# Attention and gated MLP in one kernel: a first chunk of four query tiles, a second of two, and weight low parts split between VectorE and GpSimd

## The chip, the cores and the metric

The kernel runs on one core of a Trainium2 chip. The metric is the device time of one execution in microseconds (us), the median of several runs; smaller is better.

## The reference, cut to what matters

```python
# q, k, v: (4, 8, 768, 64) float32; n_sink = 4; window = 128
scores = scale * np.matmul(q, k.transpose(0, 1, 3, 2))
is_sink = pos[None, :] < int(n_sink)
rel = pos[:, None] - pos[None, :]
in_window = (rel >= 0) & (rel < int(window))
scores = np.where(is_sink | in_window, scores, -1000000000.0)
a = np.exp(scores - max); a = a / (sum(a) + 1e-09)
attn = np.matmul(a, v)                      # sliding window and sinks
x = attn.transpose(0, 2, 1, 3).reshape(3072, 512)
out = ((x @ w_a) * (x @ w_b)) @ w_out       # 512 -> 1536 -> 512, weights float64
```

## The kernel before, in words

A query tile is 128 rows of one batch. There are 4 batches of 6 tiles, so 24 tiles, and a **chunk** is some tiles of one batch: before, eight chunks of three tiles, in the order batch 0 first half, batch 1 first half, batch 0 second half, batch 1 second half, and the same for batches 2 and 3. A chunk is written here as (batch, first tile, number of tiles).

For each chunk two things are done. **Attention** goes through 8 heads times the tiles of the chunk; one head with one tile is a **unit**. A unit's scores `s` (one window of 264 keys: 128 before, 8 sinks, 128 of its own; only 128 keys for tile 0 of a batch) are made by TensorE (PE), masked and reduced by VectorE (DVE), put through exp by ScalarE (ACT), scaled, transposed by PE, copied by ACT, and multiplied with `v` on PE (`av`); the sinks' part (`skt`, `sk`) is added once for a pair or four of heads. **MoE**, the gated product, multiplies the chunk's `x` with the weights in 12 rounds `j`: a half `a` (12 matmuls), a half `b` (12 matmuls), the product `g` (DVE), its split into a high part `gh` (ACT) and a low part `gl` (GpSimd, called POOL in the rows; in the last round DVE), and the projection `o` of the round before (9 matmuls for three tiles). Every MoE matmul is made of three: high times high, high times low, low times high.

The float64 weights are not split on the host. Each of the 36 weight tiles (`a`, `b`, `o` of 12 rounds) is loaded raw and prepared once, while it is first needed: `weight_bits` (two integer operations on DVE, L278 and L283, one conversion, L282 on ACT or L280 on GpSimd, one add on GpSimd, L285), `weight_high` (a cast on ACT, L292) and `weight_low` (a subtraction, L297, on GpSimd for the first five weights and on DVE for the other 31). All of this falls into the attention of chunk 0, which runs alone, and into the MoE of chunk 0.

The MoE of chunk c runs with the attention of chunk c+1 woven in: `between` takes steps of a generator after each half and each projection. I call this **stage c**; the attention of chunk 0 ahead of it is the **prologue**. In the prologue the first weight step is taken at step 17 of the attention and then every second step, 7 in all. Attention of chunks 0 and 1 is "exact": its matmuls take float32 operands as they are. From chunk 2 on, k, q and v are split into a high and a low part on GpSimd first (L325, L328), two instructions each. In chunk 1 heads 3, 5 and 7 have k and q split in this way too.

The order on each engine comes from a scheduler, but each engine then works strictly in its order, so an instruction that waits holds up all behind it on that engine.

Of the kernel before, what the change touches and what calls it, by code (L numbers as in the profile page):

```python
# [192 lines left out]

class Fast:
# [653 lines left out]
```

## Time and profile before

| | us |
|---|---|
| median of 3 runs | 825.75 (824.84 to 828.64) |
| the profiled execution, its own time | 826.2 |
| its span, first to last instruction | 824.4 |
| PE busy in the span | 789.7 (96%) |
| DVE busy | 439.8 (53%) |
| ACT busy | 480.0 (58%) |
| GpSimd busy | 392.9 (48%) |
| mean granted TensorE clock | 0.982 |

The busy shares are means over a span with two very different parts: the time until the weights are prepared, and the rest. They are read by stretches in what follows. A busy PE is also not a PE at its peak, since matmuls overlap and their ends are modelled; the spacing of matmul starts tells more.

### The profile page before, as it was taken

The numbers are of one execution on the slowest core, as the hardware profiler recorded it, in microseconds if no ns is written. First come the engines' busy times: TensorE is split into PE (matmuls) and PEld (weight loads), VectorE is DVE, ScalarE is ACT, GpSimd is POOL, SyncE is SP. The second block draws the span as 40 slices with busy tenths as digits, with TensorE's granted clock in tenths as the row PEclk, the third lists the DMA queues.
The fourth block names the chain that finished last, engine by engine and source line by source line (L and its number), as shares of the span: only waits on it lengthen the run. The fifth ranks groups of instructions, "written<-read, shape, count | busy, mean of one in ns | idle before, by whom it ended". The sixth has DMA issues, their size and how long they took to land.

```text
span 824.4 us, 13568 instructions
## 1 busy us (share of the span) xinstructions
PE 789.7 (96%) x4453; PEld 716.5 (87%) x4453; DVE 439.8 (53%) x1435; ACT 480.0 (58%) x1403; POOL 392.9 (48%) x469
## 2 busy tenths in 40 slices
PE   8888989989999999999999999999999999999995
PEld 5567767879999999999999999999999999999994
DVE  6999899625553456535654455535554456431001
ACT  5657757436764677647664577647775677631111
POOL 2375767736564367425545256426646256201110
PEclk9989989989999999999999999999999999999998
DMA  8855620221121133331333123332333132000001
GB/s 300 323 178 185 223 91 27 66 93 46 49 62 43 52 99 115 101 100 49 101 119 106 52 91 111 114 97 62 110 109 114 52 97 59 1 22 18 1 1 44
DMA packets 44785, 75.89 MB, mean 92 GB/s; under 512 B 4640, under 2 KB 25760, under 8 KB 44704
## 3 DMA queue, kind: packets, MB, share of 16 engines
q1 hardware_dynamic: 41648, 69.42, 26.5%
q10 hardware_dynamic: 3024, 5.51, 1.8%
q8 instruction: 37, 0.61, 0.3%
q14 instruction: 44, 0.36, 0.1%
q0 software_dynamic: 32, 0.00, 0.0%
HBM read 68.62 MB, written 6.29 MB: 91 GB/s over the span
## 4 chain that ended last, share of the span: by engine, by line
PE 80%; DVE 13%; ACT 2%; POOL 2%; issue 1%; DMA 0%; DVEq 0%; POOLq 0%; ACTq 0%
PE o L662 22%; PE b L653 21%; PE a L653 21%; PE s L399 4%; PE t L431 4%; PE av L447 4%; DVE wf_a L278 1%; PE av L576 1%; DVE w_o L297 1%; DVE wf_b L278 1%; DVE wf_a L283 1%; DVE g L674 1%; PE s L525 1%; DVE wf_o L283 1%; DVE p L533 1%
## 5 line engine op out<-in xcount | busy, mean ns | idle before, releaser
L653 PE MATMUL a<-xh,w_a 128*128 128x384 f32 x768 | 221.9, 349 | 1.2 <-DVE st L533 1.2
L653 PE MATMUL b<-xh,w_b 128*128 128x384 f32 x768 | 218.3, 345 | 0.0
L662 PE MATMUL o<-w_o,gh 128*128 128x512 f32 x576 | 188.6, 407 | 1.0 <-ACT gh L677 1.0
L679 POOL TENSOR_TENSOR gl<-g,gh 128x384 fp32r<-128x384 f32 x88 | 91.7, 1042 | 194.8 <-ACT gh L677 194.1
L653 PEld LDWEIGHTS a<-xh,w_a 128*128 128x128 f32 x768 | 142.8, 192 | 3.0 <-DVE st L533 1.4
L653 PEld LDWEIGHTS b<-xh,w_b 128*128 128x128 f32 x768 | 141.7, 190 | 0.5 <-issue 0.3
L674 DVE TENSOR_TENSOR g<-b,g 128x384 f32<-128x384 f32 x96 | 53.4, 556 | 155.3 <-PE b L653 150.9
L653 PE MATMUL a<-xl,w_a 128*128 128x384 f32 x384 | 130.9, 341 | 2.0 <-DVE xl L635 2.0
L653 PE MATMUL b<-xl,w_b 128*128 128x384 f32 x384 | 129.9, 338 | 0.0
L662 PEld LDWEIGHTS o<-w_o,gh 128*128 128x128 f32 x576 | 104.9, 190 | 19.9 <-ACT gh L677 1.8
L662 PE MATMUL o<-w_o,gl 128*128 128x512 f32 x288 | 114.9, 399 | 2.2 <-POOL gl L679 2.2
L677 ACT CAST gh<-g 128x384 fp32r<-128x384 f32 x96 | 49.3, 514 | 86.3 <-DVE g L674 86.0
L670 ACT COPY g<-a 128x384 f32<-128x384 f32 x96 | 45.2, 471 | 79.1 <-PE a L653 68.7
L410 ACT ACTIVATE p<-p,st 128x264 f32<-128x264 f32 (+1 forms) x144 | 72.2, 502 | 25.8 <-DVE st L409 24.8
L406 ACT ACTIVATE p<-p,st 128x264 f32<-128x264 f32 (+1 forms) x144 | 72.4, 503 | 9.2 <-DVE st L404 9.2
L434 ACT CAST pt<-t 128x256 fp32r<-128x256 f32 (+1 forms) x144 | 51.3, 356 | 44.5 <-PE t L431 42.8
L653 PEld LDWEIGHTS a<-xl,w_a 128*128 128x128 f32 x384 | 73.8, 192 | 3.6 <-DVE xl L635 2.3
L653 PEld LDWEIGHTS b<-xl,w_b 128*128 128x128 f32 x384 | 73.1, 190 | 0.0
L404 DVE CUSTOM_DVE_ANT_0 p<-s,mg 128x264 f32<-128x264 f32 x112 | 48.0, 429 | 45.2 <-PE s L399 45.1
L662 PEld LDWEIGHTS o<-w_o,gl 128*128 128x128 f32 x288 | 54.7, 190 | 16.0 <-POOL gl L679 2.6
L435 DVE TENSOR_TENSOR pt<-t,pt 128x256 fp32r<-128x256 f32 (+1 forms) x144 | 58.2, 404 | 18.2 <-ACT pt L434 16.7
L328 POOL TENSOR_TENSOR ks<-kr,ks 64x536 fp32r<-64x536 f32 (+1 forms) x51 | 63.9, 1254 | 4.2
(142 smaller groups left out, 1305.4 us busy)
## 6 DMA issues: line engine op xcount, KB each, us to landing
qr<-in_qT_dram SPq DMA_DIRECT2D x51, 192.0 KB, 2.4
raw_a<-in_wa_dram SPq DMA_DIRECT2D x12, 512.0 KB, 5.9
raw_b<-in_wb_dram SPq DMA_DIRECT2D x12, 512.0 KB, 6.6
raw_o<-in_wo_dram SPq DMA_DIRECT2D x12, 512.0 KB, 6.9
chk_a<-in_wa_dram SPq DMA_DIRECT2D x24, 256.0 KB, 2.7
chk_b<-in_wb_dram SPq DMA_DIRECT2D x24, 256.0 KB, 2.7
chk_o<-in_wo_dram SPq DMA_DIRECT2D x24, 256.0 KB, 2.8
out_dram<-os ACTq DMA_DIRECT2D x21, 256.0 KB, 2.1
```

Source lines behind the costliest of these rows:

```text
L328: self.nc.gpsimd.tensor_tensor(o, i, high.bitcast(F32), op=ALU.subtract)
L404: nc.vector.tensor_tensor_reduce(out=p[:, :w], in0=ps[:, :w], in1=m, scale=-0.125, scalar=BIG, op0=ALU.add, op1=ALU.min, accum_out=st[:, 0:1])
L406: nc.scalar.activation(p[:, :w], p[:, :w], AF.Exp, bias=st[:, 0:1], scale=-1.0, accum_out=st[:, 1:2])
L410: nc.scalar.mul(p[:, :w], p[:, :w], st[:, 3:4])
L434: nc.scalar.copy(hs, tp[:, :n, :])
L435: nc.vector.tensor_tensor(ls, tp[:, :n, :], hs.bitcast(F32), op=ALU.subtract)
L653: nc.tensor.matmul(ps[:, :n], lhsT=w[:, ksl], rhs=x[:, :n], start=kk == 0 and i == 0, stop=kk == NK - 1 and i == 2)
L662: nc.tensor.matmul(outs[i], lhsT=g[:, sl], rhs=w, start=j == 0 and k == 0, stop=j == NJ - 1 and k == 2)
L670: nc.scalar.copy(g[:, :n], pa[:, :n])
L674: nc.vector.tensor_tensor(g[:, :n], pb[:, :n], g[:, :n], op=ALU.mult)
L677: nc.scalar.copy(gh[:, :n], g[:, :n])
L679: e.tensor_tensor(gl[:, :n], g[:, :n], gh[:, :n].bitcast(F32), op=ALU.subtract)
```

## The change

The chunks become (0,0,4), (0,4,2), (1,0,3), (2,0,3), (1,3,3), (2,3,3), (3,0,3), (3,3,3): chunk 0 has four tiles, chunk 1 the other two of batch 0, the rest three each. In the prologue the k, q and v of two heads instead of one are loaded ahead, and the weight steps begin at step 18 and come every third step, again 7. No head of chunk 1 is split on GpSimd. Of the low parts every third weight's (all of kind `b`) goes to GpSimd, all others to DVE, and the conversion L282 is always on ACT. The copies of the sink columns `sc` go from DVE to GpSimd for chunks 0 and 1. `gl` of the last two rounds of a chunk is on DVE. In chunk 1 the transposed tile and the `av` product share one PSUM bank, since the fourth output tile of chunk 0 takes the bank `av`. The output staging tiles use the buffers of `gh` and `gl`.

```diff
-POOL_FIRST = 5
-STEP0, STEPS = 17, 2
+POOL_LOW = (1, 3)
+STEP0, STEPS = 18, 3
-SPLIT_KQ = (3, 5, 7)
+CHUNKS = ((0, 0, 4), (0, 4, 2), (1, 0, 3), (2, 0, 3), (1, 3, 3), (2, 3, 3), (3, 0, 3), (3, 3, 3))
...
-    def early(self, kind, j):
-        return 3 * j + "abo".index(kind) < POOL_FIRST
+    def low_engine(self, kind, j):
+        return self.nc.gpsimd if (3 * j + "abo".index(kind)) % POOL_LOW[1] == POOL_LOW[0] else self.nc.vector
...
-        if self.early(kind, j):
-            nc.gpsimd.tensor_scalar(lo, lo.bitcast(U32), 2.0 ** -29, 1.0, op0=ALU.mult, op1=ALU.mult)
-        else:
-            pin(nc.scalar.activation(lo, lo.bitcast(U32), AF.Copy, scale=2.0 ** -29))
+        pin(nc.scalar.activation(lo, lo.bitcast(U32), AF.Copy, scale=2.0 ** -29))
...
-        e = self.nc.gpsimd if self.early(kind, j) else self.nc.vector
+        e = self.low_engine(kind, j)
...
-                nc.vector.tensor_copy(sc[h // 2, i][:, h % 2, :], p[:, P:P + NS])
+                nc.gpsimd.tensor_copy(sc[h // 2, i][:, h % 2, :], p[:, P:P + NS])
...
-        do_prep(0)
+        for h in range(early):
+            do_prep(h)
...
-        outs = [self.ps.tile([P, DM], F32, tag=f"o{i}", name=f"o{tag}_{i}") for i in range(nt)]
+        outs = [self.ps.tile([P, DM], F32, tag=("o0", "o1", "o2", "av")[i], name=f"o{tag}_{i}") for i in range(nt)]
...
-            e = nc.vector if j == NJ - 1 else nc.gpsimd
+            e = nc.vector if j >= NJ - 2 else nc.gpsimd
...
-            o = self.mo.tile([P, DM], F32, tag="os", bufs=3, name=f"os{tag}_{i}")
+            o = self.mo.tile([P, DM], F32, tag=("gh", "gl")[i % 2], name=f"os{tag}_{i}")
...
-        chunks = [(b, t0, 3) for b0 in range(0, B, 2) for t0 in (0, 3) for b in (b0, b0 + 1)]
+        chunks = CHUNKS
...
-                gen = self.attention(nb, nt0, nnt, nxf, exact=c == 0, split=SPLIT_KQ)
+                gen = self.attention(nb, nt0, nnt, nxf, exact=c == 0)
```

GpSimd's order in the middle of stage 0, around the low part `gl` of round 5, before (`wf_o6` is the add for weight `o` of round 6; `ks`, `qh`, `ql` with 5 are the split k and q of head 5 of chunk 1):

```order
L285 TENSOR_TENSOR wf_o6_1183<-wf_o6_1183,raw_o6_985 128x512
L285 TENSOR_TENSOR wf_a7_1232<-wf_a7_1232,raw_a7_1004 128x512
L325 TENSOR_SCALAR ks1_5_0_1250<-kr1_5_0_1246 64x400
L328 TENSOR_TENSOR ks1_5_0_1250<-kr1_5_0_1246,ks1_5_0_1250 64x400
L325 TENSOR_SCALAR qh1_5_0_1251<-qr1_5_0_1248 128x384
L285 TENSOR_TENSOR wf_b7_1275<-wf_b7_1275,raw_b7_1042 128x512
L328 TENSOR_TENSOR ql1_5_0_1252<-qr1_5_0_1248,qh1_5_0_1251 128x384
L679 TENSOR_TENSOR gl0_5_1333<-g0_5_1293,gh0_5_1332 128x384
```

The same place in the changed program (`w_b6` is the low part of weight `b` of round 6, `sc` the sink copies):

```order
L689 TENSOR_TENSOR gl0_4_1297<-g0_4_1255,gh0_4_1296 128x512
L282 TENSOR_TENSOR wf_a7_1305<-wf_a7_1305,raw_a7_1113 128x512
L546 COPY sc0_4_4_0_1335<-p0_4_4_0_1328 128x8
L294 TENSOR_TENSOR w_b6_1348<-wf_b6_1237,w_b6_1348 128x512
L282 TENSOR_TENSOR wf_b7_1350<-wf_b7_1350,raw_b7_1152 128x512
L546 COPY sc0_4_4_1_1379<-p0_4_4_1_1372 128x8
L282 TENSOR_TENSOR wf_o7_1389<-wf_o7_1389,raw_o7_1180 128x512
L689 TENSOR_TENSOR gl0_5_1409<-g0_5_1368,gh0_5_1408 128x512
```

Between two `gl` there are now three adds, one low part and two small copies in every round; before there were three adds, and in three of the rounds the four operations that split a head.

GpSimd's order at the end of stage 0, before (`gl0_10` is the low part of round 10; `qh`, `ql`, `vv`, `vs` ahead of it are the last of some fourteen split operations for heads 0, 1 and 4 of chunk 2):

```order
L325 TENSOR_SCALAR vv0_1_3_2042<-vr0_0_3_2005 128x4x64
L328 TENSOR_TENSOR ql0_1_3_2037<-qr0_1_3_2033,qh0_1_3_2036 128x384
L328 TENSOR_TENSOR vv0_1_3_2042<-vr0_0_3_2005,vv0_1_3_2042 128x4x64
L325 TENSOR_SCALAR vs0_4_3_2371<-vsr0_4_3_2369 128x256
L328 TENSOR_TENSOR vs0_4_3_2371<-vsr0_4_3_2369,vs0_4_3_2371 64x256
L679 TENSOR_TENSOR gl0_10_1880<-g0_10_1849,gh0_10_1879 128x384
```

And in the changed program, the corresponding place:

```order
L325 TENSOR_TENSOR vv1_0_0_2029<-vr1_0_0_2027,vv1_0_0_2029 128x3x64
L689 TENSOR_TENSOR gl0_9_1826<-g0_9_1801,gh0_9_1825 128x512
L322 TENSOR_SCALAR vs1_0_0_2034<-vsr1_0_0_2032 128x256
L325 TENSOR_TENSOR vs1_0_0_2034<-vsr1_0_0_2032,vs1_0_0_2034 64x256
L322 TENSOR_SCALAR vv1_1_0_2064<-vr1_0_0_2027 128x3x64
L325 TENSOR_TENSOR vv1_1_0_2064<-vr1_0_0_2027,vv1_1_0_2064 128x3x64
L322 TENSOR_SCALAR qh1_1_0_2058<-qr1_1_0_2055 128x384
L294 TENSOR_TENSOR w_b11_1857<-wf_b11_1783,w_b11_1857 128x512
```

The split operations for chunk 2 stood ahead of `gl` of round 10; `gl` of round 10 is no longer on GpSimd, and the same kind of operations now stands ahead of `gl` of round 9 and of the low part `w_b11`.

## Rows read from the trace of the kernel before

**Rows 1.** Windows: length, busy of PE, PEld, DVE, ACT, POOL; clock, DMA share, GB/s.
```profile
100.00:140.00 40.00, 35.73 (x190) 31.41 (x189) 36.36 (x80) 27.02 (x67) 27.73 (x22) 0.91 0.24 74
180.00:220.00 40.00, 40.00 (x246) 37.97 (x244) 20.70 (x81) 27.01 (x82) 22.89 (x29) 1.00 0.16 43
```

**Rows 2.** Starts of rounds 1 and 11, then of stages 1, 2, 3, 4: start, us.
```profile
52.52 0.90 PE L653 MATMUL a<-xh,w_a 128*128 128x384 f32 x1
162.25 0.34 PE L653 MATMUL a<-xh,w_a 128*128 128x384 f32 x1
176.68 0.52 PE L653 MATMUL a<-xh,w_a 128*128 128x384 f32 x1
271.67 0.34 PE L653 MATMUL a<-xh,w_a 128*128 128x384 f32 x1
366.85 0.34 PE L653 MATMUL a<-xh,w_a 128*128 128x384 f32 x1
458.55 0.34 PE L653 MATMUL a<-xh,w_a 128*128 128x384 f32 x1
```

**Rows 3.** DVE's weight operations: start, us, line, operation, count.
```profile
31.12 0.69 DVE L283 SCALAR_TENSOR_TENSOR wf_b<-raw_b,wf_b 128x512 int32<-128x512 int32 x1
...
36.48 1.45 DVE L278 TENSOR_SCALAR wf_a<-raw_a 128x512 int32<-128x512 int32 x1
...
157.86 0.67 DVE L297 TENSOR_TENSOR w_b<-wf_b,w_b 128x512 fp32r<-128x512 f32 x1
```

**Rows 4.** GpSimd: an add, a low part `gl`, the split of one head.
```profile
36.37 1.28 POOL L285 TENSOR_TENSOR wf_o<-wf_o,raw_o 128x512 int32<-128x512 int32 x1
...
97.13 1.01 POOL L679 TENSOR_TENSOR gl<-g,gh 128x384 fp32r<-128x384 f32 x1 [1.98 <-ACT gh L677]
...
102.72 0.85 POOL L325 TENSOR_SCALAR ks<-kr 64x400 fp32r<-64x400 f32 x1
103.66 1.13 POOL L328 TENSOR_TENSOR ks<-kr,ks 64x400 fp32r<-64x400 f32 x1
104.87 0.83 POOL L325 TENSOR_SCALAR qh<-qr 128x384 fp32r<-128x384 f32 x1
...
107.35 1.20 POOL L328 TENSOR_TENSOR ql<-qr,qh 128x384 fp32r<-128x384 f32 x1
```

**Rows 5.** DVE groups until 177 us: count, busy us, mean ns, idle before.
```profile
L297 DVE TENSOR_TENSOR w_a<-wf_a,w_a 128x512 fp32r<-128x512 f32 x10 | 10.0, 1005 | 0.0
...
L547 DVE COPY sc<-p 128x8 f32<-128x8 f32 x16 | 5.6, 351 | 2.0 <-ACT p L542 1.9
```

**Rows 6.** Chain that ended last: start, us, line, matmuls in the piece.
```profile
11.27 1.24 PE av L576 x10
...
13.44 0.45 PE s L525 x2
13.88 0.11 PE t L562
...
189.60 2.08 PE a L653 x12
...
195.48 2.11 PE o L662 x9
...
389.91 0.59 PE av L447 x5
```

**Rows 7.** The prologue on DVE: first unit, first weight step.
```profile
6.39 0.29 DVE L533 CUSTOM_DVE_ANT_0 p<-s,m 128x128 f32<-128x128 f32 x1
...
26.65 0.41 DVE L278 TENSOR_SCALAR wf_a<-raw_a 128x512 int32<-128x512 int32 x1
```

**Rows 8.** End of stage 0 on GpSimd and on PE.
```profile
168.16 0.99 POOL L679 TENSOR_TENSOR gl<-g,gh 128x384 fp32r<-128x384 f32 x1
...
169.21 0.50 PE L662 MATMUL o<-w_o,gl 128*128 128x512 f32 x1 [2.17 <-POOL gl L679]
```

**Rows 9.** Windows: stage 3, columns as in rows 1.
```profile
366.80:458.50 91.70, 91.63 (x531) 85.43 (x531) 46.27 (x175) 57.36 (x180) 45.02 (x63) 1.00 0.31 93
```

More of the change, by code (lines that the diff above doesn't have):

```diff
@@ L369, in prep_v, with attention @@
         return vv
-    def attention(self, b, t0, nt, xf, exact=False, split=(), alone=False):
-        parts = self.parts_exact(b, t0, nt, xf, split, alone) if exact else self.parts_split(b, t0, nt, xf)
+    def attention(self, b, t0, nt, xf, exact=False, alone=False):
+        parts = self.parts_exact(b, t0, nt, xf, alone) if exact else self.parts_split(b, t0, nt, xf)
         late = [i for i in range(nt) if t0 + i >= 2]
         units = [(h, i) for h in range(H) for i in range(nt)]
-        return self.pipeline(units, nt, late, *parts, 3 if alone else 2, 2 if exact else 4)
+        return self.pipeline(units, nt, late, *parts, 3 if alone else 2, 2 if exact else 4, 2 if alone else 1)
     def parts_split(self, b, t0, nt, xf):
@@ L476, in parts_split, with parts_exact @@
         return do_prep, scores, transposes, av, sinks_t, sinks_av
-    def parts_exact(self, b, t0, nt, xf, split, alone):
+    def parts_exact(self, b, t0, nt, xf, alone):
         nc = self.nc
@@ L523, in scores @@
             ps = self.ps.tile([P, SW], F32, tag="sa"[n % 2] if alone else "s", name=f"s{u}")
[L524 to L526 removed]
+            nc.tensor.matmul(ps[:, :w], lhsT=q[:, i * P:(i + 1) * P], rhs=k[:, c0:c0 + w], start=True, stop=True)
             if alone and n % 5 > 2:
@@ L590, in sinks_av, with pipeline @@
             n = len(late)
-            ps = self.ps.tile([P, 3 * P], F32, tag="av", name=f"sk{tag}_{pr}")
-            nc.tensor.matmul(ps[:, :n * P], lhsT=vss[pr], rhs=skt.pop(pr)[:, :n * P], start=True, stop=True)
-            xs = xf[pr][:, late[0] * P:nt * P]
-            nc.vector.tensor_tensor(xs, ps[:, :n * P], xs, op=ALU.add)
+            if alone:
+                ps = self.ps.tile([P, 4, P], F32, tag="av", name=f"sk{tag}_{pr}")
+            else:
+                ps = half_bank(1, f"sk{tag}_{pr}")
+            nc.tensor.matmul(ps[:, :n, :], lhsT=vss[pr], rhs=skt.pop(pr)[:, :n * P], start=True, stop=True)
+            xs = xf[pr][:, late[0] * P:nt * P].rearrange("p (c q) -> p c q", q=P)
+            nc.vector.tensor_tensor(xs, ps[:, :n, :], xs, op=ALU.add)
         return do_prep, scores, transposes, av, sinks_t, sinks_av
-    def pipeline(self, units, nt, late, do_prep, scores, transposes, av, sinks_t, sinks_av, lag, group):
-        do_prep(0)
+    def pipeline(self, units, nt, late, do_prep, scores, transposes, av, sinks_t, sinks_av, lag, group, early):
+        for h in range(early):
+            do_prep(h)
         yield
@@ L712, in run @@
         b, t0, nt = chunks[0]
-        xf = self.new_xf(0)
+        pairs = [self.wp.tile([P, 2, nt * P], F32, tag=f"w_{k}{NJ - 1}", name=f"xf0_{k}") for k in "bo"]
+        xf = [x[:, i, :] for x in pairs for i in range(2)]
         first = self.attention(b, t0, nt, xf, exact=True, alone=True)
```

116 lines of the change are left out of this document (60 added, 56 removed).

## The prediction

> **What bounds the kernel now.** I read the windows first. From 100 to 140 us DVE is busy 36.4 of 40 us and PE's clock is granted at 0.91 on average, so it partly ran at the lower of its two levels; from 180 to 220 us DVE is busy 20.7, PE all 40 and the clock is full [rows 1]. So there are two regimes: PE bounds the kernel from the end of stage 0 on, and before that PE waits for prepared weights. Then the starts of rounds: in stage 0 ten rounds take 162.25 - 52.52 = 109.7 us, 10.97 each; stage 1 takes 271.67 - 176.68 = 95.0, stage 2 95.2 and stage 3 91.7 us [rows 2]. Stage 3 is shorter because the attention woven into it is of tiles 0 to 2, whose first tile has half a window; stages 1 and 2 carry tiles 3 to 5. The end of stage 0 shows one wait of its own: PE stands 2.17 us for `gl` of round 10, which GpSimd does at 168.16, behind the split operations of chunk 2 [rows 8]. From the start of round 11 to stage 1 it takes 14.4 us [rows 2].
>
> What a round costs PE comes from the chain: 12 matmuls of 384 columns 2.08 us (0.173 each), 9 of 512 columns 2.11 (0.234 each), 5 of 256 columns 0.59 (0.118 each) [rows 6]. A round of three tiles is 2 x 2.08 + 2.11 = 6.27 us, and twelve are 75.2. Exact attention costs 0.45 us for scores, 0.22 for two transposes and 0.124 for each of the `av` matmuls [rows 6]. In stage 0 before, 24 units (a third of them tile 0, at half) and 80 `av` matmuls make about 2.0 us per round, the sinks a little more, so PE had some 8.5 us of work in a round of 10.97: over a fifth of stage 0 was waiting or ran at the lower clock.
>
> **What sets the 10.97.** DVE's share says DVE, but its durations say something finer. L278 takes 0.41 us in one place and 1.45 in another [rows 3, 7]; the long one began at 36.48, just after GpSimd's add began at 36.37 (1.28 us), and ended after it [rows 3, 4]. I therefore count the pair as one resource, with the time that each operation takes alone. A round before: GpSimd three adds 3 x 1.28, `gl` 1.01, and the split of three heads (0.85 + 1.13 + 0.83 + 1.20 = 4.01 each) spread over some eleven rounds, 1.09: 5.9 us. DVE three times 0.41 + 0.69 + 0.67: 5.3 us [rows 3, 4, 7]. Together 11.2, against 10.97 measured: the two engines' sum, not DVE alone, fills the round.
>
> The Trainium skill has the rule for it ("SBUF — State Buffer", section "SBUF: two separate sides"): VectorE and GpSimd share one pair of SBUF ports, taken as a lock for a whole instruction, and the other engine blocks. It speaks against this change: a low part moved to GpSimd frees DVE but holds the lock longer. The stretched L278 agrees with it. By it a round would need the 11.3 us of the next part; by DVE's mean durations alone, the 9.7 of the first rival.
>
> **The change, part by part.**
>
> *Prologue.* The first unit reaches DVE at 6.39 us, the first weight operation, at step 17, at 26.65: 1.19 us per step [rows 7]. Eight units more (32 for 24), with the same 7 weight steps spread between them, put the end of the prologue 8 x 1.19 = 9.5 us later, and round 1 at 52.5 + 9.5 = 62.0. The copies `sc` leave DVE, but a tile 0 is now one unit in four instead of one in three; I let these cancel. Larger loads, two heads ahead, cost nothing here: behind each head lie four steps of 1.19 us. If that cover failed, a head would be late by a step or two, 1 to 2 us. The conversion L282 of the first five weights goes from GpSimd, which is nearly idle there, to ACT, which waits for DVE in the prologue: nothing.
>
> *Stage 0, PE.* A round of four tiles: 24 x 0.234 + 12 x 0.234 = 8.4 us (I take the 512-column row for the halves too). Chunk 1 now has 16 units: 16 x 0.67 + 8 heads x 8 `av` matmuls x 0.124 + 4 pairs of sinks, 0.65 us each as an estimate from the scores row, make 21.3 us, 1.8 per round. Together 10.2 us.
>
> *Stage 0, DVE and GpSimd.* GpSimd: three adds and one low part 4 x 1.28 (a subtraction of the same shape as an add), `gl` 1.01 x 4/3 = 1.35, sink copies 0.2 (1.3 per round, between nothing and DVE's mean of 0.35 each [rows 5]), no head to split: 6.7. DVE: 3 x (0.41 + 0.69) + 2 x 0.67 = 4.6. Together 11.3, as much as before. The low part on GpSimd costs 1.28 for 0.67, the heads that are no longer split pay for it. So the period is bounded below by PE at 10.2, and the shared account gives 11.3 x 10.97/11.2 = 11.1. With both nearly full, and each waiting for the other once a round, I take 11.3. Round 11 then starts at 62 + 113 = 175.0.
>
> *End of stage 0.* Rounds 11 and the rest of 10: 24 x 0.234 for the halves, 24 x 0.234 for two projections, 11.2 us, and 1 us that I choose for the handover. `gl` of round 10 on DVE removes the 2.17 us wait. In its place `w_b11` stands behind the split of chunk 2 on GpSimd, two heads of 4.0 us for k and q alone [rows 4]; its add is a good round of 11 us ahead of its use, so I cost it at nothing; without that cover PE's third matmul of the last half `b` waits for up to one head, 4 us. Stage 1 starts at 187.2, 10.5 us later than before.
>
> *Stage 1.* Two tiles: 24 x 0.118 + 6 x 0.234 = 4.24, twelve rounds 50.8. Attention and all small losses of a stage with tiles 0 to 2 are 91.7 - 75.2 = 16.5 (stage 3). Sum 67.3; the same attention in a shorter stage leaves less slack, for which I add 2: 69.3 instead of 95.0, so 25.7 us less.
>
> *Stages 2 to 7.* The same kinds of stages in another order (before three with tiles 3 to 5 and two with tiles 0 to 2, after the same), so nothing. Output tiles in the buffers of `gh` and `gl` cost nothing: the next chunk writes its first `gh` after two halves, 4.2 us [rows 6], and the stores have that long; without that cover perhaps 1 us per chunk. `gl` of round 10 on DVE is hidden from stage 1 on, where DVE is half idle [rows 1].
>
> Sum: 826.2 + 10.5 - 25.7 = 811.0 against the profiled execution's own time, which is 0.45 us above the median of the runs shown; I leave that out. In short: 25 us of MoE work for PE move from stage 1 into a stretch where PE was waiting, and a longer prologue gives some of it back.
>
> **The rivals.**
>
> *PE alone sets stage 0* (period 10.3). For it: by the means, DVE gets lighter. Of 31 low parts in stage 0 it keeps 22, 0.75 fewer per round at 1.0 us; 0.67 fewer copies at 0.35 [rows 5]; 0.67 fewer units at some 0.8 (an estimate from the 1.19 of a prologue step); wider `g` and `gl` add 0.2. That is 10.97 - 0.75 - 0.23 - 0.54 + 0.2 = 9.7, below PE's 10.2. Against it: the means contain the waiting for GpSimd. 10 rounds x 1.0 less: 801.
>
> *The relief isn't one.* Each half `b` now waits at its third matmul for a low part on GpSimd, which stands behind an add and in front of two others and `gl`; both engines wait in turn, and the period is 12.3, as if the 1.28 of a low part came on top of the present 10.97. For it: the account above is full; against it: the low part is due a whole round ahead. 10 us more: 821.
>
> *Stage 1 too dense.* ACT has 57.4 us of work in the 91.7 of stage 3 [rows 9]. In 69 us that would be 83% instead of 63%. If ACT worked at 75% there, the stage would be 77 us: 819. Against it: part of the 57.4 is on wider `g` and on weight checks, which stage 1 has not.
>
> *Slower.* The mechanism is GpSimd's strict order in stage 0: a sink copy or a low part waits for its producer, and the adds behind it wait too, so DVE lacks the buffer for the next weight. The break-even period is 11.3 + 15.2/10 = 12.8; at 13.4 it is 832. For it: each round of GpSimd's order has more waits in it than before. Against it: its own work in a round is 6.7 of 11.3.
>
> **How the numbers follow.** The main case 0.50 (its own range 805 to 817), PE alone 0.17, no relief 0.17, stage 1 too dense 0.07, slower 0.09. A change of about 0.5% (4 us) is what a measurement can tell. Faster by more: 0.50 + 0.17 + 0.07 and half of 0.17, 0.82. Within 0.5%: 0.09, mostly the other half. Slower: 0.09. The range 799 to 823 reaches from PE alone to no relief, and leaves out the slower case and the tails.
>
> **What would show each step.** Round 1 at 62 us, round 11 at 175, stage 1 from 187 to 256, each within a few us; later stages of 91.7 and 95 as before. In stage 0, PE's mean spacing in a half at 0.234, DVE still above 85% busy, and PE busy enough that the clock stays full. Long L278 rows still next to GpSimd adds would show that the shared account holds; L278 rows at 0.41 throughout would show it wrong. The prediction is wrong if the period leaves 10.2 to 12.3, if `w_b` low parts or sink copies appear as what PE waits for by more than a few us, or if stage 1 takes over 78 us.

## The result and the profile after

The changed kernel takes 816.11 us (median of 4 runs, 814.39 to 817.08), the kernel before 827.19 us beside it (824.84 to 829.45). The ratio is 0.9864, 95% interval 0.9844 to 0.9885: faster by 11 us, where 15 were forecast (811.0). The profiled execution of the changed kernel has a span of 812.5 us and a mean granted clock of 0.993; before it was 824.4 us and 0.982. Of the kernels run further below, one execution of a3 took 860.87 us at a mean granted clock of 0.85; it is in a3's median (810.88, without it 810.40) and not in its ratio.

The same starts as in [rows 2], changed kernel (the first matmul of half `a`): rounds 1, 3 and 11 of stage 0, then stages 1, 2 and 3.

```profile
60.74 0.50 PE L663 MATMUL a<-xh,w_a 128*128 128x512 f32 x1
...
88.96 0.40 PE L663 MATMUL a<-xh,w_a 128*128 128x512 f32 x1
...
178.12 0.40 PE L663 MATMUL a<-xh,w_a 128*128 128x512 f32 x1
...
189.32 0.28 PE L663 MATMUL a<-xh,w_a 128*128 128x256 f32 x1
...
258.05 0.34 PE L663 MATMUL a<-xh,w_a 128*128 128x384 f32 x1
...
351.24 0.34 PE L663 MATMUL a<-xh,w_a 128*128 128x384 f32 x1
```

Stage 1 ends a little later than the start of stage 2 says. PE's timeline at that place (start, us, operation, count):

```profile
258.05 0.34 PE L663 MATMUL a<-xh,w_a 128*128 128x384 f32 x1
258.23 1.16 PE L672 MATMUL o<-w_o,gh 128*128 128x512 f32 x4
259.22 0.63 PE L672 MATMUL o<-w_o,gl 128*128 128x512 f32 x2
259.69 0.34 PE L663 MATMUL a<-xl,w_a 128*128 128x384 f32 x1
```

Six projections of stage 1 stand behind the first matmul of stage 2, 1.4 us. So stage 1 took 258.05 - 189.32 + 1.4 = 70.1 us, and stage 2 is 91.8, not the 93.2 between the starts. With that, the forecast's terms against the trace (us; the rows called long are lengths, the others changes against the kernel before):

| | forecast | measured | difference |
|---|---|---|---|
| prologue, to round 1 | +9.5 | 60.74 - 52.52 = +8.2 | -1.3 |
| rounds 1 and 2 | 22.6 long | 28.2 long | +5.6 |
| rounds 3 to 10 | 90.4 long | 89.2 long | -1.2 |
| round 11 to stage 1 | 12.2 long | 11.2 long | -1.0 |
| stage 1 | 69.3 long | 70.1 long | +0.8 |
| the rest | 0 | +0.3 | +0.3 |
| sum, as the change of the span | -15.2 | -11.9 | +3.3 |

Rounds 1 and 2 alone miss by 5.6 us, and the other terms win 2.3 us of it back. Windows of the changed kernel (columns as in [rows 1]): the first window of [rows 1]; round 2; its second part; rounds 3 to 10; stage 1.

```profile
100.00:140.00 40.00, 38.69 (x181) 28.90 (x180) 30.44 (x61) 25.46 (x59) 24.25 (x25) 1.00 0.23 70
70.00:89.00 19.00, 13.73 (x54) 10.34 (x53) 17.11 (x29) 10.37 (x25) 14.63 (x14) 0.82 0.52 184
82.00:89.00 7.00, 7.00 (x25) 5.15 (x26) 5.55 (x14) 5.49 (x14) 4.28 (x6) 0.64 0.37 152
88.96:178.12 89.16, 87.85 (x409) 66.82 (x408) 64.76 (x116) 50.81 (x112) 62.22 (x61) 1.00 0.22 68
189.30:258.00 68.70, 66.71 (x489) 62.06 (x488) 38.44 (x158) 46.84 (x146) 41.18 (x62) 1.00 0.22 66
```

From 100 to 140 us DVE is busy 30.4 of 40, not 36.4 as in [rows 1], PE 38.7, and the clock is full. From round 3 to round 10 PE stands only 1.3 us in 89.2. Round 2, 19 us long, is different: DVE busy 17.1, PE 13.7, the clock 0.82. What happens there is read on three engines side by side. DVE's timeline, complete from 74.40 to 81.58:

```profile
74.40 1.54 DVE L278 TENSOR_SCALAR wf_a<-raw_a 128x512 int32<-128x512 int32 x1
75.97 1.65 DVE L280 SCALAR_TENSOR_TENSOR wf_a<-raw_a,wf_a 128x512 int32<-128x512 int32 x1
77.54 0.68 DVE L294 TENSOR_TENSOR w_a<-wf_a,w_a 128x512 fp32r<-128x512 f32 x1
78.14 1.48 DVE L278 TENSOR_SCALAR wf_b<-raw_b 128x512 int32<-128x512 int32 x1
79.66 1.65 DVE L280 SCALAR_TENSOR_TENSOR wf_b<-raw_b,wf_b 128x512 int32<-128x512 int32 x1
81.23 0.42 DVE L532 CUSTOM_DVE_ANT_0 p<-s,mg 128x264 f32<-128x264 f32 x1
```

GpSimd's, complete from 73.89 to 80.76:

```profile
73.89 1.76 POOL L282 TENSOR_TENSOR wf_o<-wf_o,raw_o 128x512 int32<-128x512 int32 x1
75.60 1.47 POOL L689 TENSOR_TENSOR gl<-g,gh 128x512 fp32r<-128x512 f32 x1
77.02 0.65 POOL L546 COPY sc<-p 128x8 f32<-128x8 f32 x1
77.63 1.71 POOL L294 TENSOR_TENSOR w_b<-wf_b,w_b 128x512 fp32r<-128x512 f32 x1
79.31 1.45 POOL L282 TENSOR_TENSOR wf_a<-wf_a,raw_a 128x512 int32<-128x512 int32 x1
```

And PE's, from the last matmul ahead of the gap (in brackets how long PE stood, and for whom):

```profile
76.06 0.39 PE L663 MATMUL b<-xh,w_b 128*128 128x512 f32 x1
81.72 1.25 PE L525 MATMUL s<-kx,qx 128*128 128x264 f32 x2 [5.26 <-DVE st L532]
82.89 1.97 PE L579 MATMUL t<-ptx,vx 128*64 128x128 f32 x8
```

Put the ends of DVE's and GpSimd's operations side by side. The add on GpSimd ends at 75.65; L278, begun at 74.40, ends at 75.94, 0.3 us behind it (alone it takes 0.41). `gl` ends at 77.07, L280 at 77.62; the low part `w_b` ends at 79.34, L278 at 79.62; the add ends at 80.76, L280 at 81.31. L280, 0.69 us alone, ends 0.55 us behind in both cases. Each of the four long DVE operations thus ends a little less than its own length after the GpSimd operation that stood in its way, and the five operations ahead of L532, which take 0.4 to 0.7 us each alone, fill 6.8 us. Behind them, in DVE's strict order, stands L532, which empties the one PSUM bank of scores; PE's next scores need that bank, and everything else on PE stands behind these scores: 5.26 us. The stretched rows are what "SBUF — State Buffer" of the Trainium skill, section "SBUF: two separate sides", states (the lock is held for a whole instruction), and the trace agrees. After the gap the granted clock is 0.64 from 82 to 89 us, a mean between the full level (2.4 GHz) and the lower one (1.2 GHz), and the eight `av` matmuls take 1.97 us. Eight of them later, at the full clock in the same timeline:

```profile
98.51 1.09 PE L579 MATMUL t<-ptx,vx 128*64 128x128 f32 x8
```

### The profile page after: what moved, and what is told of

The parts are those of the page before. It is cut to its first block, busy times and chain, and to the rows that moved or that the text cites. A ratio compares the mean times of both kernels' runs of the same rounds, so it can differ in the third digit from the quotient of the medians.

```text
span 812.5 us, 13593 instructions
## 1 busy us (share of the span) xinstructions
PE 788.8 (97%) x4457; PEld 698.6 (86%) x4457; DVE 432.7 (53%) x1427; ACT 476.7 (59%) x1384; POOL 380.7 (47%) x483
## 4 chain that ended last, share of the span: by engine, by line
PE 85%; DVE 8%; ACT 3%; issue 2%; POOL 0%; DMA 0%; DVEq 0%; POOLq 0%; ACTq 0%
PE o L672 23%; PE a L663 23%; PE b L663 22%; PE t L428 4%; PE s L396 4%; PE av L444 3%; PE s L525 2%; PE av L579 1%; PE t L562 1%; PE t L579 1%; DVE p L539 1%; DVE wf_a L280 1%; DVE wf_a L278 1%; DVE g L684 1%; ACT p L403 1%
## 5 line engine op out<-in xcount | busy, mean ns | idle before, releaser
L663 PE MATMUL a<-xh,w_a 128*128 128x384 f32 (+2 forms) x768 | 218.9, 346 | 0.0
L663 PE MATMUL b<-xh,w_b 128*128 128x384 f32 (+2 forms) x768 | 215.3, 343 | 0.0
L689 POOL TENSOR_TENSOR gl<-g,gh 128x384 fp32r<-128x384 f32 (+2 forms) x80 | 82.8, 1035 | 197.5 <-ACT gh L687 194.7
L684 DVE TENSOR_TENSOR g<-b,g 128x384 f32<-128x384 f32 (+2 forms) x96 | 53.4, 556 | 152.6 <-PE b L663 144.5
L663 PE MATMUL a<-xl,w_a 128*128 128x384 f32 (+2 forms) x384 | 129.3, 337 | 0.9 <-DVE xl L645 0.9
L663 PE MATMUL b<-xl,w_b 128*128 128x384 f32 (+2 forms) x384 | 129.1, 336 | 0.0
L407 ACT ACTIVATE p<-p,st 128x128 f32<-128x128 f32 (+1 forms) x144 | 71.4, 496 | 26.4 <-DVE st L406 25.5
L403 ACT ACTIVATE p<-p,st 128x128 f32<-128x128 f32 (+1 forms) x144 | 71.6, 497 | 8.4 <-DVE st L401 8.3
L431 ACT CAST pt<-t 128x128 fp32r<-128x128 f32 (+1 forms) x144 | 50.4, 350 | 39.3 <-PE t L428 37.5
L432 DVE TENSOR_TENSOR pt<-t,pt 128x128 fp32r<-128x128 f32 (+1 forms) x144 | 57.2, 397 | 21.1 <-ACT pt L431 19.5
L672 PEld LDWEIGHTS o<-w_o,gl 128*128 128x128 f32 x288 | 54.3, 189 | 14.1 <-POOL gl L689 1.0
L325 POOL TENSOR_TENSOR ks<-kr,ks 64x400 fp32r<-64x400 f32 (+1 forms) x48 | 57.6, 1200 | 3.9
```

What stands on the lines that cost most here:

```text
L325: self.nc.gpsimd.tensor_tensor(o, i, high.bitcast(F32), op=ALU.subtract)
L403: nc.scalar.activation(p[:, :w], p[:, :w], AF.Exp, bias=st[:, 0:1], scale=-1.0, accum_out=st[:, 1:2])
L407: nc.scalar.mul(p[:, :w], p[:, :w], st[:, 3:4])
L431: nc.scalar.copy(hs, tp[:, :n, :])
L432: nc.vector.tensor_tensor(ls, tp[:, :n, :], hs.bitcast(F32), op=ALU.subtract)
L663: nc.tensor.matmul(ps[:, :n], lhsT=w[:, ksl], rhs=x[:, :n], start=kk == 0 and i == 0, stop=kk == NK - 1 and i == 2)
```

## The experiments

Theory A, the prediction's: DVE and GpSimd, excluding each other, set all of stage 0. Theory B, formed from the trace above: they do so only until the weights that fell behind are caught up (about 82 us); from round 3 on PE itself is the bound, at a price per round that the forecast set too low. The runs with their main times (starts from the trace, us):

| kernel | median | ratio to before, interval | round 1 | round 3 | round 11 | stage 1 |
|---|---|---|---|---|---|---|
| before | | | 52.5 | 74.9 | 162.2 | 176.7 |
| changed | 816.11 | 0.9864 (0.9844 to 0.9885) | 60.7 | 89.0 | 178.1 | 189.3 |
| a1 low parts on DVE | 812.99 | 0.9832 (0.9811 to 0.9852) | 62.5 | 89.8 | 177.9 | 189.1 |
| a2 `gl` on DVE | 813.84 | 0.9840 (0.9822 to 0.9857) | 63.6 | 91.2 | 178.5 | 189.7 |
| a3 both | 810.88 | 0.9810 (0.9794 to 0.9825) | 59.8 | 85.4 | 172.8 | 184.0 |
| a6 shares as before | 812.56 | 0.9827 (0.9810 to 0.9844) | 59.3 | 86.7 | 175.3 | 186.5 |
| a7 adds on DVE | 811.85 | 0.9820 (0.9802 to 0.9837) | 62.1 | 83.9 | 174.5 | 185.7 |
| a8 a3 and copies on DVE | 810.01 | 0.9801 (0.9785 to 0.9817) | 57.3 | 83.9 | 173.5 | 184.7 |
| c1 a3, less weight lead | 811.21 | 0.9818 (0.9802 to 0.9833) | 59.0 | 86.9 | 174.2 | 185.4 |
| e1 more matmuls | 822.23 | 0.9949 (0.9934 to 0.9964) | 60.9 | 89.1 | 183.9 | 195.1 |
| a4 chunks of three | 817.73 | 0.9891 (0.9875 to 0.9907) | 46.9 | 72.0 | 158.6 | 169.8 |
| b1 before, `gl` of round 10 on DVE | 823.55 | 0.9961 (0.9947 to 0.9976) | 53.3 | 75.7 | 164.0 | 173.8 |
| d1 one head ahead | 815.44 | 0.9867 (0.9851 to 0.9883) | 59.0 | 88.1 | 177.2 | 188.4 |
| d2 conversions on GpSimd | 818.03 | 0.9896 (0.9880 to 0.9913) | 61.4 | 92.1 | 181.4 | 192.6 |

The kernel before took 826.65 to 827.19 us (median) beside them. One profiled execution is one sample: the changed kernel's, with 814.39 us, is the shortest of its four. Differences of 1 to 2 us between two kernels' starts are therefore not read alone. An edit can also change the order of the other operations on an engine, as it does in d2 below, so a difference in round 2 is not always the edited operation's own. DVE has begun 17 weights when round 3 starts in the changed kernel, a2, d2 and e1, 16 in a1, a6, c1 and d1, and 15 in a3, a7 and a8; round 3 starts at 89.0 to 92.1, 86.7 to 89.8 and 83.9 to 85.4 us in these three groups.

### a1, a2, a3: GpSimd relieved of low parts, of `gl`, of both

```diff
 def low_engine(self, kind, j):                      # a1, a3
-    return self.nc.gpsimd if (3 * j + "abo".index(kind)) % POOL_LOW[1] == POOL_LOW[0] else self.nc.vector
+    return self.nc.vector
...
-            e = nc.vector if j >= NJ - 2 else nc.gpsimd                    # a2, a3
+            e = nc.vector if row == 0 or j >= NJ - 2 else nc.gpsimd
```

a1: 

> The changed kernel with every weight low part on DVE and none on GpSimd. Shared account (DVE and GpSimd exclude each other): a round loses 1.28 us of GpSimd and gains 0.67 of DVE, so the period of 11.74 us falls to about 11.1 and the time by about 6 us, to some 810. Rival, DVE alone is the bound: DVE gets three quarters of an operation of 1.0 us more per round, the period rises to about 12.5 and the time by 7 us, to some 823.

a2: 

> The changed kernel with gl of all rounds of stage 0 on DVE (as it is in the last two rounds). Shared account: a round loses 1.3 us of GpSimd and gains 0.68 of DVE, period about 11.1, time 6 us less, some 810. DVE alone as the bound: period up by 0.7 us or more, time 7 us more, some 823.

a3: 

> Both edits together: low parts and gl of stage 0 all on DVE, GpSimd keeps the adds and the sink copies. Shared account: 11.3 - 0.6 - 0.65 = 10.05 us per round, now below PE's 10.2, so the period is PE's with some waiting, 10.4 to 10.8, and the time about 10 us less, some 806. DVE alone as the bound: period over 13, time 14 us more, some 830.

Measured: 812.99, 813.84 and 810.88. All three put more work on DVE and none is slower; a3's interval lies wholly below the changed kernel's, the other two overlap with it. The 823 to 830 us that DVE's own load as the bound would have given are refuted. How little DVE is charged for it shows in a2. Rounds 1 to 10 of the changed kernel, then of a2, in windows:

```profile
60.74:178.12 117.38, 110.21 (x497) 83.92 (x497) 91.06 (x156) 67.52 (x147) 84.06 (x79) 0.97 0.31 106
```

```profile
63.60:178.50 114.90, 109.68 (x497) 84.02 (x497) 88.26 (x166) 67.43 (x147) 71.06 (x69) 0.97 0.32 110
```

DVE has ten operations more (166 for 156) and its busy time fell, from 91.1 to 88.3 us. The groups of DVE in these stretches (count, busy us, mean ns) say why; first the changed kernel, then a2:

```profile
L278 DVE TENSOR_SCALAR wf_a<-raw_a 128x512 int32<-128x512 int32 x9 | 11.4, 1267 | 0.0
...
L689 DVE TENSOR_TENSOR gl<-g,gh 128x512 fp32r<-128x512 f32 x1 | 1.8, 1773 | 0.0
```

```profile
L689 DVE TENSOR_TENSOR gl<-g,gh 128x512 fp32r<-128x512 f32 x11 | 11.2, 1017 | 4.5 <-ACT gh L687 4.5
...
L278 DVE TENSOR_SCALAR wf_a<-raw_a 128x512 int32<-128x512 int32 x9 | 6.0, 662 | 0.0
```

`gl` costs DVE 9.4 us more, and one group of waiting L278 gives back 5.4 of it. But the relief does not appear where theory A has it. In a3, rounds 1 and 2 together with the prologue lose 3.5 us (round 3 starts at 85.4 instead of 89.0) and rounds 3 to 10 only 1.8. In a3 PE does not stand at all in them:

```profile
85.43:172.79 87.36, 87.36 (x409) 66.88 (x408) 66.03 (x135) 51.85 (x114) 42.41 (x47) 1.00 0.22 70
```

GpSimd is busy 42.4 us there instead of 62.2, and the eight rounds still take 10.9 each. That is theory B.

### e1: is PE the bound from round 3 on?

```diff
-                for k, (g, w) in enumerate(((gh, wh), (gh, wl), (gl, wh))):
+                gw = ((gh, wh), (gh, wl), (gl, wh)) + (((gh, wh),) if row == 0 and 0 < j < NJ - 2 else ())
+                for k, (g, w) in enumerate(gw):
```

> The changed kernel with four more matmuls of 512 columns per round (the first pass of the `o` projection is issued twice) in rounds 2 to 10 of stage 0. It changes the output of the first chunk. Price on TensorE: 4 x 0.234 = 0.94 us per round, 8.4 us in nine rounds; no other engine gets any work. The prediction's theory (DVE and GpSimd set the period in all of stage 0, TensorE has 10.2 of 11.3): the additions fit in, and the time moves by 0 to 2 us. The revised theory (the pair bounds only until about 82 us, TensorE from round 3 or 4 on): rounds 2 and 3 hide them, rounds 4 to 10 grow by 0.9 each, and the time rises by 6 to 8 us, to about 822 to 824.

Measured: 822.23 us, 6.1 more than the changed kernel; the ratio's interval leaves no overlap. Rounds 3 to 10 of e1:

```profile
89.10:183.95 94.85, 94.85 (x442) 72.81 (x440) 64.33 (x116) 49.99 (x111) 61.85 (x61) 1.00 0.21 62
```

Round 3 starts where it did (89.10 for 88.96): rounds 1 and 2 hide the added work, PE waits there. Rounds 3 to 10 grow from 89.16 to 94.85, 5.7 us: 0.9 to 1.0 in each of rounds 3, 4, 6, 8, 9 and 10, and nothing in rounds 5 and 7, which were 11.8 us long and stay so. These two are the ones that a2 and a3 shorten to 10.9. In the changed kernel PE stands 0.66 us in round 5 and 0.65 us in round 7, for a copy of ACT's; PE's timeline in round 5:

```profile
113.18 0.44 PE L562 MATMUL t<-ident,p 128*128 128x128 f32 x2 [0.66 <-ACT xf L581]
```

In ACT's order that copy stands behind an exp, the exp waits for L532 on DVE, and L532 stands behind L294 (1.65 us, against 0.67 alone) and L278 (1.49), which ran beside GpSimd's add and `gl`. So theory B, with 2 x 0.9 us left for theory A in eight rounds.

### a7: the adds on DVE

```diff
-        nc.gpsimd.tensor_tensor(f, f, lo, op=ALU.add)
+        nc.vector.tensor_tensor(f, f, lo, op=ALU.add)
```

> The changed kernel with the weight's last addition (L282, 1.28 us or more on GpSimd) on DVE. It leaves out the exact integer sum: DVE adds in floating point, so the low bits of a weight differ. Shared account: an addition on DVE takes about 0.7 us alone instead of 1.28 on GpSimd, and with GpSimd left with low parts, `gl` and copies (about 3 us per round) the long rows of L278 go to 0.41; three additions per round save some 1.7 us of the sum of both engines. Where the pair is the bound (the prologue and rounds 1 to 3) this shows: the 19.0 us round falls to 11 to 13; in rounds 4 to 9, where PE had no gaps, nothing moves. Time 803 to 808. If DVE alone is the bound, its load per round rises by 2 us and the time is 825 or more.

Measured: 811.85, against 803 to 808 by the one and 825 by the other. The long round is gone as the shared account has it, though DVE's order also differs (15 weights begun before round 3, not 17): rounds 1 and 2 take 21.8 instead of 28.2 us, and PE's wait at that place is 0.86 us. PE's timeline in a7, and the window from 60 to 90 us in which the changed kernel's PE was busy 24.15 us at a clock of 0.89:

```profile
78.01 0.71 PE L525 MATMUL s<-kx,qx 128*128 128x264 f32 x2 [0.86 <-DVE st L532]
```

```profile
60.00:90.00 30.00, 27.35 (x122) 21.26 (x123) 28.69 (x56) 20.34 (x45) 10.92 (x12) 1.00 0.77 283
```

But rounds 3 to 10 grow by 1.5 us (90.7 for 89.2): rounds 4, 6 and 8 take 13.5, 13.1 and 12.3 us instead of 12.0, 12.1 and 11.6. In rounds 4 and 6 PE waits 1.36 and 0.96 us for L592, a copy of DVE's for the sinks, which stands behind all the operations of a weight's bits in DVE's order, the add now among them; in round 8 it waits 0.50 us for another DVE operation. PE's and DVE's timelines in round 4 of a7:

```profile
97.67 0.44 PE L562 MATMUL t<-ident,p 128*128 128x128 f32 x2 [1.36 <-DVE sct L592]
```

```profile
93.86 1.52 DVE L278 TENSOR_SCALAR wf_a<-raw_a 128x512 int32<-128x512 int32 x1
95.42 0.69 DVE L280 SCALAR_TENSOR_TENSOR wf_a<-raw_a,wf_a 128x512 int32<-128x512 int32 x1
96.24 0.69 DVE L282 CUSTOM_DVE_ANT_0 wf_a<-raw_a,wf_a 128x1024 uint16<-128x1024 uint16 x1
96.85 0.43 DVE L532 CUSTOM_DVE_ANT_0 p<-s,mg 128x264 f32<-128x264 f32 x1
97.20 0.08 DVE L532 DVE_READ_ACCUMULATOR2_ANT st<- 128x1 f32 x1
97.20 0.41 DVE L592 COPY sct<-t 16x256 f32<-16x256 f32 x1
```

The expectation that all L278 rows would fall to 0.41 was wrong too: `wf_a` still has a mean of 1.05 us, since GpSimd keeps `gl` and the low parts.

### a6 and a8: the other shares, and the best version

```diff
-        return self.nc.gpsimd if (3 * j + "abo".index(kind)) % POOL_LOW[1] == POOL_LOW[0] else self.nc.vector
+        return self.nc.gpsimd if 3 * j + "abo".index(kind) < 5 else self.nc.vector      # a6; a8: always vector
...
-                nc.gpsimd.tensor_copy(sc[h // 2, i][:, h % 2, :], p[:, P:P + NS])
+                nc.vector.tensor_copy(sc[h // 2, i][:, h % 2, :], p[:, P:P + NS])        # a6 and a8
...
-            e = nc.vector if j >= NJ - 2 else nc.gpsimd
+            e = nc.vector if j == NJ - 1 else nc.gpsimd            # a6; a8: as in a3
```

a6: 

> The changed kernel with the old shares of the two engines: the first five low parts on GpSimd and 31 on DVE, sink copies on DVE, `gl` of round 10 on GpSimd. Chunks of four and two tiles, the early loads and the conversions on ACT stay. Shared account (DVE and GpSimd one resource where both are the bound): GpSimd loses nine more low parts and 0.2 us of copies per round, DVE gains them, so rounds 1 to 3 lose some of their 19.0 us outlier as in the kernel with all low parts on DVE, -2 to -3 us; the `gl` of round 10 gives 2 us back at the end of each stage where GpSimd splits heads; sum 812 to 816. If DVE alone were the bound, nine low parts by 0.9 us and some 60 copies by 0.35 us in stage 0 would cost DVE about 2.9 us per round and the time would be above 825.

a8: 

> The changed kernel with all low parts, `gl` of stage 0 and the sink copies on DVE: GpSimd keeps the weights' additions alone there. By the pair's account a copy costs less on DVE (0.35 us) than on GpSimd (0.65 us as it stands in a row of the changed kernel's trace), so with some eight copies until 82 us this is 0 to 3 us faster than the kernel with low parts and `gl` alone on DVE (808.0 us of span in its own profile), and no later round moves. If DVE's own busy time is the bound by then, eight copies of 0.35 us make it 2 to 3 us slower.

Measured: 812.56 and 810.01. With the old shares of the engines the changed kernel is some 3 us faster (816.11 x (0.9864 - 0.9827) / 0.9864; the intervals just touch): giving GpSimd every third low part and the copies, and DVE the `gl` of round 10, gained nothing and seems to cost time. a8 is the fastest kernel of the study. Its interval lies wholly below that of the changed kernel, about 5 us faster; against a3 it can't be told apart.

In a6 PE has no wait for `gl` of round 10 although that is on GpSimd again, and round 11 to stage 1 takes 11.2 us as in the changed kernel. GpSimd begins it at 174.80 there, ahead of round 11's first matmul at 175.35; in the kernel before it began 5.9 us after that matmul [rows 2, 8]. The 2 us that the expectation gave back did not appear.

### b1: `gl` of round 10 alone, in the kernel before

```diff
-            e = nc.vector if j == NJ - 1 else nc.gpsimd
+            e = nc.vector if j >= NJ - 2 else nc.gpsimd
```

> The kernel before, with one edit of the change alone: `gl` of round 10 on DVE instead of GpSimd, in all eight stages. If the wait of 2.17 us that PE had for this `gl` ended the path, stage 0 from round 11 on takes about 11 to 12 us instead of 14.4, and the time falls by 2 to 3 us, to about 824. If the rest of chunk 2's preparation on GpSimd or DVE was due just as late, the wait only changes its name and the time stays at that of the kernel before (within 1 us). Rounds 1 to 10 should not move by either.

Measured: 823.55, ratio 0.9961 (0.9947 to 0.9976): 3.2 us. Round 11 to stage 1 in windows, first the kernel before, then b1:

```profile
162.25:176.68 14.43, 11.23 (x44) 8.93 (x43) 3.04 (x7) 3.81 (x8) 6.66 (x10) 0.78 0.42 124
```

```profile
164.00:173.80 9.80, 8.79 (x44) 7.40 (x43) 5.96 (x8) 3.80 (x8) 6.81 (x9) 1.00 0.58 156
```

The stretch shrinks by 4.6 us, twice the wait of 2.17 us [rows 8]: without the wait the clock also stays at 1.00 instead of 0.78. (Round 11 began 1.8 us later in this one profile; nothing in the edit touches what lies ahead of it.)

### a4: the chunks of three with the other edits

```diff
-CHUNKS = ((0, 0, 4), (0, 4, 2), (1, 0, 3), (2, 0, 3), (1, 3, 3), (2, 3, 3), (3, 0, 3), (3, 3, 3))
+CHUNKS = ((0, 0, 3), (0, 3, 3), (1, 0, 3), (2, 0, 3), (1, 3, 3), (2, 3, 3), (3, 0, 3), (3, 3, 3))
```

With it chunk 1's transposes and `av` use PSUM banks of their own again.

> The changed kernel with chunks (0,0,3), (0,3,3) in place of (0,0,4), (0,4,2); all else as changed. If the chunk sizes are what gains, by filling PE in stage 0: the prologue is 9.5 us shorter, the period stays near 11 us (the two engines set it, although PE has only 8.8 us of work in a round), stage 1 is 24 us longer; the time is about 823, as much as before the change or a few us less. Rival, the gain comes from the moves between engines and the period follows PE's work: period 10.3, time about 814, no worse than the changed kernel.

Measured: 817.73, ratio 0.9891. Without chunks of four and two, most of the gain is still there; the sizes themselves are worth 0.9891 - 0.9864, some 2 us (the intervals overlap by 0.001), 3.0 in the profiled spans (815.5 and 812.5). Neither theory's time was met; the period, 111.7 / 10 = 11.2 us, is that of the first theory. From a4 to the changed kernel the start of round 1 moves from 46.9 to 60.7 (+13.8), rounds 1 to 10 take 117.4 for 111.7 (+5.7), and stage 1 shrinks from 91.5 to 70.1 (-21.4). So 19.5 of 21.4 us are paid back in the prologue and stage 0. From before to a4, on the other hand, round 1 begins 5.6 us earlier (7 weights begun by then instead of 8), round 11 to stage 1 takes 11.2 instead of 14.4, and stage 1 takes 91.5 instead of 95.0, since the attention woven into it is now of tiles 0 to 2; that of tiles 3 to 5 went into stage 0.

How much there was to fill shows in rounds 1 to 10 of the kernel before and of a4:

```profile
52.52:162.25 109.73, 97.21 (x507) 83.84 (x505) 99.32 (x207) 72.05 (x180) 73.94 (x60) 0.93 0.39 130
```

```profile
46.95:158.64 111.69, 101.58 (x541) 82.79 (x539) 97.77 (x196) 75.94 (x184) 84.28 (x81) 0.98 0.37 129
```

PE stands 12.5 us before and 10.1 us in a4; in the changed kernel, with a fourth tile, it still stands 7.2 of 117.4.

### d1, d2, c1: parts that were priced at nothing

```diff
-        return self.pipeline(units, nt, late, *parts, 3 if alone else 2, 2 if exact else 4, 2 if alone else 1)
+        return self.pipeline(units, nt, late, *parts, 3 if alone else 2, 2 if exact else 4, 1)     # d1
...
-        pin(nc.scalar.activation(lo, lo.bitcast(U32), AF.Copy, scale=2.0 ** -29))
+        if 3 * j + "abo".index(kind) < 5:                                                          # d2
+            nc.gpsimd.tensor_scalar(lo, lo.bitcast(U32), 2.0 ** -29, 1.0, op0=ALU.mult, op1=ALU.mult)
+        else:
+            pin(nc.scalar.activation(lo, lo.bitcast(U32), AF.Copy, scale=2.0 ** -29))
...
-STEP0, STEPS = 18, 3
-AHEAD, LOADS = 3, 9
+STEP0, STEPS = 18, 4                                                                               # c1, on a3
+AHEAD, LOADS = 2, 9
```

d1: 

> The changed kernel with the inputs of the first attention one head ahead instead of two. The prediction gave this part of the change nothing, since behind each head lie four steps of 1.19 us; then round 1 begins where it does in the changed kernel (60.7 us, within 1 us) and the time stays at 816. Rival: the loads were late in the prologue before (there a head lay three steps ahead), and the two heads are what made the prologue shorter than forecast; then round 1 begins 2 to 6 us later and the time rises by 1 to 5 us.

d2: 

> The changed kernel with the conversion L279 of the first five weights on GpSimd again instead of ACT. The prediction gave this nothing. By the pair's account five conversions on GpSimd, at about the duration of an addition, block DVE for some 6 us in the prologue; round 1 begins 3 to 6 us later than at 60.7 us, and the time rises by 2 to 5 us. If GpSimd is idle enough there, round 1 stays within 1 us and the time at 816.

c1: 

> The changed kernel with all low parts and `gl` of stage 0 on DVE (808.0 us of span in its own profile), and with fewer weights prepared ahead: one weight step in four units of the prologue instead of three, and a lead of two weights instead of three. The theory that the prologue and the first rounds pay for a debt of weight work on DVE and GpSimd: the prologue gets shorter by one to two weight steps of 1.2 us, the first rounds wait for as much, and the total moves by -2 to +1 us against that kernel. If the lead is what hides GpSimd's additions from PE, each of rounds 1 to 10 waits for its weight, the period rises by 0.5 us or more, and the time is 5 us or more above it.

Measured: d1 815.44, no difference from the changed kernel: two heads ahead buy nothing that these runs can tell. d2 818.03, some 2.6 us slower by the ratios (the intervals overlap by 0.0005), 3.1 in the spans. Round 1 begins only 0.6 us later, round 3 3.1 us later. The five conversions themselves ran on GpSimd from 16.5 to 26.0 us, 3.7 us in all, 35 us ahead of round 1. What differs is round 2. PE's and DVE's timelines in d2:

```profile
88.17 0.69 PE L565 MATMUL t<-ident,p 128*128 128x128 f32 x2 [8.20 <-ACT xf L584]
```

```profile
66.73 0.42 DVE L535 CUSTOM_DVE_ANT_0 p<-s,mg 128x264 f32<-128x264 f32 x1
...
86.52 0.68 DVE L687 TENSOR_TENSOR g<-b,g 128x512 f32<-128x512 f32 x1
```

Round 2 takes 21.6 us. By their count the two masked scores that DVE does at 81.23 and 84.26 in the changed kernel are done at 58.81 and 66.73 here (L535), ahead of the weight operations; but `g` stands behind them, at 86.52 and not at 83.66. PE stands 8.20 us for a copy of ACT's, which stands behind `gh`, which waits for that `g`. So we read d2's loss as that of another order of DVE around the same six weights; what the conversions cost by themselves on GpSimd is not shown. c1 811.21 against a3's 810.88, no difference: weight work taken out of the prologue returns in rounds 1 to 3 (round 1 0.8 us earlier, round 3 1.5 us later). That fits a debt that is paid before round 3, at whatever place.

## Why the forecast came out as it did

**Direction and the main case: right. The mechanism of stage 0: right in two rounds, wrong in eight.** The step that failed is "What sets the 10.97", carried over as one period of 11.3 us, a sum of DVE and GpSimd, for ten rounds. The runs show two regimes. Until round 3 PE waits for DVE, whose weight operations GpSimd lengthens, as the rows of round 2 show, and rounds 1 and 2 took 28.2 us. Relieving GpSimd shortens them to 25.7 us with more work on DVE (a3) and to 21.8 (a7), but in both DVE also begins two weights fewer before round 3, and in a2, with `gl` moved and as many weights begun, round 3 starts no earlier. How much of the wait is the lengthening and how much the number of weights that DVE's order puts ahead was not tried apart. The forecast spread the weight work evenly, 3 weights per round; between the starts of rounds 2 and 3 of the changed kernel six weights are begun, in no other round more than four, and five of their operations stand ahead of the one that PE waits for. Per weight the forecast was not too cheap: ten weights begun in 28.2 us are 2.8 us each, where it had 11.3 / 3 = 3.8. From round 3 on PE is the bound (e1), and GpSimd's relief moves it by 1.8 us in eight rounds (a3).

**The agreement of 11.2 with 10.97 was luck.** The sum counts DVE's weight operations alone. In rounds 1 to 10 of the kernel before DVE was busy another 28.8 us with attention and `g`, 2.9 us per round, which the sum leaves out; and 10.97 was itself a mean of rounds of 8.4 to 16.5 us, as the starts in that trace show.

**That rounds 3 to 10 came out at 11.15 against 11.3 is two errors that cancel.** PE's own work was put at 10.2. Eight rounds of 8.4 us of MoE are 67.2; 89.2 less these and the 1.3 us that PE stood leave 20.7, 2.6 us of attention per round and not 1.8. The forecast divided 21.3 us by twelve rounds, but the weaving is ahead of the MoE and ends in round 10: by the forecast's own prices the attention matmuls in these eight rounds (11 units' scores, 13 units' transposes, 56 `av`, 4 pairs of sinks) make 17.4 us, 2.2 per round. The other 0.4 per round is more than the rows of single matmuls price. So the rival "PE alone sets stage 0" had the mechanism of these rounds, with a period of 10.3 that was too short.

**Prologue.** 60.7 against 62.0. To the first matmul of round 0 it is 47.37 against 38.40 us in the kernel before, 9.0 us for eight units, so the 1.19 us per unit held. Round 0 itself takes 13.4 us, 14.1 before and 9.0 in a4; the forecast had no term for it. "The conversion goes from GpSimd, which is nearly idle there, to ACT: nothing": undoing it costs 2 to 3 us (d2), but by another order in round 2, so the step is neither confirmed nor refuted. Two heads ahead: nothing, right (d1).

**The low part on GpSimd.** Its price was 1.28 us; the trace until 178 us has a mean of 1.53, beside the adds at 1.37 to 1.40. The groups of GpSimd in the changed kernel:

```profile
L294 POOL TENSOR_TENSOR w_b<-wf_b,w_b 128x512 fp32r<-128x512 f32 x12 | 18.4, 1529 | 7.9 <-ACT w_b L289 7.9
...
L689 POOL TENSOR_TENSOR gl<-g,gh 128x512 fp32r<-128x512 f32 x10 | 14.6, 1459 | 1.4 <-ACT gh L687 1.4
```

The step counted the move as paid for by the heads that are no longer split; taken back by itself it is worth some 2.6 us by the ratios (a1; the intervals overlap by 0.0008); taken back together with `gl` it is 4.5 us (a3), and with the copies too some 5 us (a8). That the rule in the Trainium skill speaks against this part of the change was right.

**End of stage 0.** The wait of 2.17 us is gone, as forecast, and the stretch is shorter by 3.2 instead of 2.2 us: the clock came back with the wait (b1). In the changed kernel the edit may not be what does it, since a6, with the other old shares too, has no wait without it; undoing it alone was not tried. `w_b11` behind the split of chunk 2 cost nothing, as forecast.

**Stage 1.** 70.1 against 69.3. Of the two losses that were named, ACT is busy 46.8 of 68.7 us, 68%, and was no bound. The 25 us moved as forecast; what the forecast's "a stretch where PE was waiting" got wrong is how much of it the prologue and stage 0 give back (a4): 19.5 of 21.4 us. The forecast saw over a fifth of stage 0 free, some 25 us; PE stood 12.5 us in rounds 1 to 10 of the kernel before.

**So the total is right partly by luck.** By the forecast's own terms the chunk sizes were worth 9.6 us (+9.5 for the prologue, 10 x (11.3 - 10.97) = +3.3 for the rounds, 69.3 - 91.7 = -22.4 for stage 1), and all else 5.5 us (2.2 at the end of stage 0, 95.0 - 91.7 = 3.3 for the order of the chunks). In the spans the sizes brought 3.0 us and all else 8.9 (a4). These 8.9 lie mainly in round 0 (5.1 us shorter), in the end of stage 0 (3.3 us, a4 and b1) and in stage 1 with tiles 0 to 2 (3.5 us), less 2.0 us in rounds 1 to 10 and 1.5 us in the later stages.

**Named signs.** Long L278 rows beside GpSimd's: there. DVE above 85% busy: no, 76% from 100 to 140 us. PE waiting for `w_b` or for copies: no; it waited for the score bank, behind stretched weight operations, a wait that the forecast did not name. The clock: full from round 3 on, 0.82 in round 2. Later stages unchanged: yes, 0.3 us.

**What stays open.** How much of the 5.6 us by which a4's round 1 begins earlier comes from the one weight fewer was not tried apart, nor the changed kernel with an order of DVE in which both L532 and `g` stand ahead of the weight operations of round 2 (in d2 L532 does, `g` does not). Not run either: the changed kernel with fewer weights ahead of round 3 and nothing else moved, and the kernel before with the chunk sizes alone.

## What to carry to other kernels

Two engines that exclude each other are one resource only where they are the bound: find from which round on the consumer has no gaps, and price the rounds before and after apart. Before that, work on the slower of the two delays the other, even where it looks idle in the mean; test with moves in both directions, and look whether the order of the other operations moved too. And when a mean period fits, add a known amount of work to the supposed idle engine: one run with 0.94 us more per round showed what the sum could not.
